# Attention with projected keys, then a two-branch maximum network: the loads of batch 0's v and of two weight matrices, each made in two transfers

## The chip, the core and the metric

The kernel runs on one core of a Trainium2 chip. A core has a matrix engine (TensorE, "PE" in the profile, with its weight loads as "PEld"), a vector engine (VectorE, "DVE"), a scalar engine (ScalarE, "ACT"), GpSimd ("POOL") and a queue engine (SyncE, "SP"). SP, ACT and POOL also issue transfers between the chip's memory and the on-chip memory (SBUF, 128 partitions); sixteen DMA engines carry them out. The metric is the device time of one execution in microseconds, as the median of several runs.

## What is computed

Eight batches of eight heads, 1,024 positions, head size 64. Keys and values are projected along the positions to 64 rows by E and F, softmax attention follows, and its output goes through two matrices, an elementwise maximum, and a third matrix:

```python
k_proj = np.einsum('ks,bhsd->bhkd', E, k)
v_proj = np.einsum('ks,bhsd->bhkd', F, v)
scores = scale * np.matmul(q, k_proj.transpose(0, 1, 3, 2))
scores = scores - np.max(scores, axis=-1, keepdims=True)
attn = np.exp(scores)
attn = attn / (np.sum(attn, axis=-1, keepdims=True) + 1e-09)
attn_out = np.matmul(attn, v_proj)
...
h1 = x @ w1
h2 = x @ w2
g = np.maximum(h1, h2)
return (g @ w_out).astype(np.float32)
```

x is the attention output as 8,192 rows of 512; w1 and w2 are 512 x 1,024, w_out is 1,024 x 512. All inputs are float32 in memory.

## The kernel before

The kernel computes in float16. The maximum is rewritten: max(h1, h2) = relu(h1 - h2) + h2, so that the second layer is relu(x wd) w_out + x m, with wd = w1 - w2 (`step_wd`, `step_wd_rows`) and m = w2 w_out (`m_steps`). For m, w2 is first transposed on TensorE (`step_w2t`). From batch 1 on, the products are made by a scheme of seven smaller products in place of eight, for which sums and differences of blocks are prepared on VectorE (`sums_x`, `sums_g`, `step_t`, `step_tw`).

The work is laid out by hand in one order for all engines; each engine runs its own instructions in the order in which they were written, and waits where data is missing. The batch is the outer unit. Batch 0 is the fill: its attention is done piece by piece while its inputs and the weights come in, with idle matmuls (`warm`) in the first 18 us to keep TensorE busy.

The loads of q, k, v and of the weights are issued from GpSimd, since they turn float32 into float16 on their way. They stand in this order: two heads of k are fetched by SP; then from GpSimd the other two heads of the first half of k, the first half of q, the second half of k, the second half of q; then batch 0's v in four loads of two heads (256 KB in SBUF each); then fourteen loads of pieces of w2 and w1 (128 KB each, two of them 256 KB), here called chunks 0 to 13; then w_out (1 MB), and batch 1's k, v, q and batch 2's k. Chunks 0 to 3 are columns 0 to 255 of w2 and w1, half of the rows each; 4 and 5 are columns 256 to 511 of w2, 6 and 7 the same of w1; 8 and 9 columns 512 to 1,023 of w2; 10 and 11 columns 512 to 767 of w1; 12 and 13 the rest of w1. A semaphore tells when a load has landed. GpSimd's loads use eight semaphores in turn.

How the loads are used: `step_kv` projects v (L195) as its four loads land. `step_wd` takes w1 - w2 of columns 0 to 255 from chunks 0 to 3 and of columns 256 to 511 from chunks 4 to 7 (DVE, L540); `step_wd_rows` does the columns from 512 on, one half of the rows at a time, from chunks 8 to 13 (L548). `up_slots` multiplies batch 0's x by wd, a block of 128 columns at a time (L524); `step_w2t` transposes w2 (L556), 256 columns at a time. Then `m_steps` needs w_out (L633), `step_t` makes its block differences (L596), and `down_steps` is the second layer (L837). Batch 1's k and v are projected at L237.

Of the kernel before, what the change touches and what calls it, by code (L numbers as in the profile page):

```python
# [19 lines left out]
def kernel(  # L20
# [12 lines left out]
    nc = tc.nc  # L33
# [5 lines left out]
    NC = S // 128  # L39
# [25 lines left out]
    def mm_bank(dtype=FP32, n=None):  # L65
        if n is None:
            n = turn.pop(0)
            turn.append(n)
        return ps.tile([128, 512 if dtype == FP32 else 1024], dtype, tag=f"mm{n}", name="mm_ps")
# [37 lines left out]
    def load(t, n, src, b, h0, h1):  # L107
        nc.gpsimd.dma_start(  # L108
            out=t[n][:, h0:h1],
            in_=src[b, h0:h1].rearrange("h (p c) d -> p h c d", c=NC),  # L110
        )

    tiles = {b: {} for b in range(B)}
    for n in ("k", "q", "v"):
        alloc(tiles[0], n)
# [4 lines left out]
                ident = const.tile([128, 128], FP32)  # L120
                make_identity(nc, ident)
    for h in range(0, H, 2):
        load(tiles[0], "v", v, 0, h, h + 2)

    w1_sb = big(1).rearrange("p (r f) -> p r f", r=NDC)
    w2_sb = big(2).rearrange("p (r f) -> p r f", r=NDC)
    wo_sb = const.tile([128, NFB, DM], FP16, tag="wo", name="wo_sb")
    for g in range(2):
        for w_sb, w in ((w2_sb, moe_w2), (w1_sb, moe_w1)):
            nc.gpsimd.dma_start(  # L130
                out=w_sb.rearrange("p (g z) f -> p g z f", z=2)[:, g, :, 0:256],
                in_=w.rearrange("(g p z) f -> p g z f", p=128, z=2)[:, g, :, 0:256],
            )
    for w_sb, w, f0, f1 in (
        (w2_sb, moe_w2, 256, 512), (w1_sb, moe_w1, 256, 512), (w2_sb, moe_w2, 512, DF),
        (w1_sb, moe_w1, 512, 768), (w1_sb, moe_w1, 768, DF),
    ):
        for z in range(2):
            nc.gpsimd.dma_start(
                out=w_sb.rearrange("p (g z) f -> p g z f", z=2)[:, :, z, f0:f1],  # L140
                in_=w.rearrange("(g p z) f -> p g z f", p=128, z=2)[:, :, z, f0:f1],
            )
    nc.gpsimd.dma_start(out=wo_sb, in_=moe_w_out.rearrange("(r p) f -> p r f", p=128))

# [866 lines left out]
    f = lambda s, *a: lambda: s(tiles[0], *a)  # L1011
# [72 lines left out]
    for n, x in enumerate((  # L1084
# [4 lines left out]
        for name in x.split():  # L1089
# [6 lines left out]
            else:  # L1096
                g, j = int(name[2]), int(name[3])
# [38 lines left out]
    for i, (new, old) in enumerate(zip([*groups[1:], none], groups)):  # L1136
        n, h = divmod(i + 2, 2)
# [54 lines left out]
    for reg in regs:  # L1192
# [4 lines left out]
        out=mm_bank()[0:1, 0:1], lhsT=ones16[:, 0:1], rhs=ones16[:, 0:1], start=True, stop=True  # L1197
# [166 lines left out]
```

## Time and profile before

| | us |
|---|---|
| median of 3 runs | 320.39 |
| lowest and highest run | 320.32, 322.92 |
| span of the profiled execution | 318.1 |
| TensorE busy in it | 312.3 |
| VectorE busy | 241.1 |
| ScalarE busy | 206.2 |
| GpSimd busy | 40.8 |

The span is the time from the first to the last instruction of one profiled execution; the runs' times are taken around it. The granted clock of TensorE was 1.000 over the span. The profile has these views: busy times by engine; the chain of work that ended last, followed backwards from the last instruction; windows, which give each engine's busy time in stretches of the span; timelines by engine; and, for a tile, its instructions, who waited for them, and how long its transfers took from issue to landing. In a timeline a row has its start, its length, engine, line, operation, the tile written and the one read, how many instructions are merged in it, and in brackets the idle time of the engine before it and what ended that. Several weight tiles appear under the name "big"; `v_sb`, `k_sb`, `q_sb` are the inputs, `wd_sb` is w1 - w2, `wo_sb` is w_out. The length of a transfer's row on GpSimd or SP is what the issue took, not the transfer. The DMA share is the mean busy share of the sixteen DMA engines, and exceeds 1 where packets overlap.

### The profile page before, as it was taken

The page shows a single profiled execution, that of the slowest core. Times are in us where ns is not written, and L with a number is a line of the kernel's source. Part 1 is how long each engine was busy: PE and PEld are TensorE (multiplying, and loading weights), DVE is VectorE, ACT ScalarE, POOL GpSimd, SP SyncE. Part 2 cuts the span into 40 slices and gives each one's busy share as a digit, 9 for nine tenths or more (in the row PEclk, how much of TensorE's full clock was granted, in tenths as well). Part 3 has the DMA queues.
Part 4 walks back from the last instruction along what each step waited for, and adds up shares of the span by engine and source line. Part 5 has one row for each costly group of instructions (what it writes and reads, how often), then busy time and mean ns, then how long its engine had stood idle before and what let it go on. Part 6 is the DMA issues. An engine that isn't in the chain of part 4 may idle for free.

```text
span 318.1 us, 9308 instructions
## 1 busy us (share of the span) xinstructions
PE 312.3 (98%) x3922; PEld 253.6 (80%) x3922; DVE 241.1 (76%) x441; ACT 206.2 (65%) x373; POOL 40.8 (13%) x63
## 2 busy tenths in 40 slices
PE   8989999999999999999999999999999999999996
PEld 3555588888887888788887888788887888888885
DVE  2366888877969696996969696996969696969883
ACT  2476842777776777477776778477776777765541
POOL 8259002003000300022000400030000000000000
PEclk9999999999999999999999999999999999999999
DMA  7999999999979999899999999989979131313124
GB/s 189 206 200 195 207 206 202 207 158 160 204 139 195 162 212 245 210 182 154 223 233 217 167 204 245 215 151 183 232 149 209 45 102 36 102 35 102 36 99 136
DMA packets 76684, 53.71 MB, mean 169 GB/s; under 512 B 29664, under 2 KB 76128, under 8 KB 76640
## 3 DMA queue, kind: packets, MB, share of 16 engines
q0 software_dynamic: 30688, 28.05, 56.0%
q1 hardware_dynamic: 45664, 24.85, 32.7%
q8 instruction: 31, 0.51, 0.6%
q10 hardware_dynamic: 288, 0.20, 0.2%
q14 instruction: 13, 0.11, 0.1%
HBM read 57.15 MB, written 16.78 MB: 232 GB/s over the span
## 4 chain that ended last, share of the span: by engine, by line
PE 92%; DMA 5%; POOL 1%; ACT 1%; issue 0%; DVE 0%; POOLq 0%
PE mm_ps L837 47%; PE mm_ps L745 27%; PE mm_ps L524 4%; DMA v_sb<-in_v_dram 4%; PE att_ps L352 3%; PE mm_ps L195 3%; PE mm_ps L340 2%; PE mm_ps L633 2%; PE att_ps L237 1%; DMA out_dram<-o_sb 1%; PE mm_ps L311 1%; POOL k_sb L108 0%; POOL q_sb L108 0%; ACT ld_sb L388 0%; ACT ex_sb L380 0%
## 5 line engine op out<-in xcount | busy, mean ns | idle before, releaser
L719 ACT COPY p_sb<-mm_ps 128x512 f32<-128x512 f32 x179 | 101.8, 592 | 49.1 <-PE mm_ps L745 27.2
L837 PEld LDWEIGHTS <-big 128*128 128x128 f16 x768 | 73.5, 98 | 11.8 <-issue 3.6
L837 PE MATMUL mm_ps<-T_sb,big 128*128 128x256 f16 x576 | 76.9, 273 | 0.0
L760 DVE TENSOR_TENSOR gt_sb<-mm_ps,p_sb 128x512 f16<-128x512 f32 x56 | 38.5, 687 | 43.0 <-PE mm_ps L745 41.6
L745 PE MATMUL mm_ps<-big,big 128*128 128x256 f16 x336 | 50.4, 273 | 0.0
L745 PEld LDWEIGHTS <-big 128*128 128x128 f16 x448 | 43.8, 98 | 5.1
L837 PE MATMUL mm_ps<-wo_sb,gt_sb 128*128 128x256 f16 x256 | 42.6, 273 | 0.0
L837 PEld LDWEIGHTS <-gt_sb 128*128 128x128 f16 x376 | 35.7, 98 | 6.7 <-issue 2.7
L469 ACT ACTIVATE ex_sb<-mm_ps 128x512 f16<-128x512 f32 x50 | 27.2, 596 | 18.0 <-PE mm_ps L340 12.3
L745 PEld LDWEIGHTS <-wd_sb 128*128 128x128 f16 x336 | 32.9, 98 | 3.8
L745 PE MATMUL mm_ps<-xt_sb,wd_sb 128*128 128x256 f16 x224 | 32.8, 273 | 0.0
L499 DVE TENSOR_TENSOR xt_sb<-att_ps,ld_sb 128x1024 f16<-128x1024 f32 x26 | 31.7, 1219 | 0.2
L837 PE MATMUL mm_ps<-m_sb,xt_sb 128*128 128x256 f16 x128 | 24.4, 273 | 0.0
L303 POOL COPY junk<-qt_sb 1x1 f16<-1x1 f16 x6 | 2.1, 346 | 172.5 <-DMA qt_sb<-q_sb 172.5
L868 DVE TENSOR_TENSOR o_sb<-mm_ps,p_sb 128x512 f32<-128x512 f32 x32 | 21.9, 683 | 2.8 <-ACT p_sb L897 2.0
L763 DVE TENSOR_SCALAR gt_sb<-gt_sb 128x512 f16<-128x512 f16 (+1 forms) x60 | 20.9, 348 | 2.1
L705 DVE TENSOR_TENSOR big<-gt_sb 128x1024 f16<-128x1024 f16 x32 | 21.8, 683 | 0.0
L837 PE MATMUL mm_ps<-wo_sb,big 128*128 128x256 f16 x128 | 21.5, 273 | 0.0
L806 ACT ACTIVATE gt_sb<-mm_ps 128x512 f16<-128x512 f32 x28 | 16.8, 601 | 5.7 <-PE mm_ps L745 5.7
L837 PE MATMUL mm_ps<-T_sb,gt_sb 128*128 128x256 f16 x120 | 20.3, 273 | 0.0
L837 PEld LDWEIGHTS <-xt_sb 128*128 128x128 f16 x188 | 18.3, 98 | 2.3 <-issue 0.2
L760 DVE TENSOR_TENSOR gt_sb<-p_sb 128x512 f16<-128x512 f32 x28 | 19.1, 682 | 0.6 <-ACT p_sb L719 0.6
(121 smaller groups left out, 434.7 us busy)
## 6 DMA issues: line engine op xcount, KB each, us to landing
out_dram<-o_sb SPq DMA_DIRECT2D x62, 256.0 KB
k_sb<-in_k_dram POOLq DMA_DIRECT2D x7, 1024.0 KB, 9.8
v_sb<-in_v_dram POOLq DMA_DIRECT2D x7, 1024.0 KB, 15.3
q_sb<-in_q_dram POOLq DMA_DIRECT2D x5, 1024.0 KB, 23.0
q_sb<-in_q_dram POOLq DMA_DIRECT2D x6, 512.0 KB, 15.8
big<-in_moe_w_dram POOLq DMA_DIRECT2D x12, 128.0 KB, 6.3
v_sb<-in_v_dram POOLq DMA_DIRECT2D x4, 256.0 KB, 13.6
wo_sb<-in_moe_w_out_dram POOLq DMA_DIRECT2D x1, 1024.0 KB, 10.4
```

The costliest lines, as they stand in the source:

```text
L195: nc.tensor.matmul(out=kv_ps[r * KP : (r + 1) * KP, h * D : (h + nh) * D], lhsT=eft[i][:, c, :], rhs=t[w][:, h0 + h : h0 + h + nh, c, :], ...
L469: nc.scalar.activation(out=t["ex", g, j][:, e, :], in_=banks[e], func=ACTF.Exp, scale=scale)
L499: nc.vector.tensor_tensor(out=x_out(t, g, j).rearrange("q z o n -> q o z n"), in0=at_ps.rearrange("q o (z n) -> q o z n", z=2), in1=ld[:, ...
L524: nc.tensor.matmul(out=h_ps, lhsT=wd_sb[:, r, fb * 128 : (fb + 1) * 128], rhs=t["xt"][:, r, :, j * W : (j + 1) * W], start=(r == 0), stop= ...
L705: nc.vector.tensor_tensor(out=S(i), in0=S(0) if x is None else x, in1=y(), op=op)
L719: copy(out=x, in_=bank)
L745: nc.tensor.matmul(out=bank[:, m * W : (m + 1) * W], lhsT=w_[:, n_, (2 * d + m) * 128 : (2 * d + m + 1) * 128], rhs=a[:, n_, :], start=(n ...
L760: nc.vector.tensor_tensor(out=c_blk(j, c), in0=two(x), in1=two(y), op=ALU.add)
L763: nc.vector.tensor_scalar_max(ap, ap, 0.0)
L806: nc.scalar.activation(out=out, in_=in_, func=ACTF.Relu)
L837: nc.tensor.matmul(out=bank[i][:, 0:CH] if two_banks else bank[:, i * CH : (i + 1) * CH], lhsT=a(c)[:, i * 128 : (i + 1) * 128], rhs=w_(c) ...
L868: nc.vector.tensor_tensor(out=o_sb, in0=two(x), in1=two(y), op=ALU.add)
```

## The change

A helper `load_parts` makes a load as two transfers: of partitions 0 to 119, and of partitions 120 to 127. Batch 0's v and all chunks of w1 and w2 go through it. Their order, and all other loads, are as before. The four loads of v become eight, the fourteen chunks twenty-eight transfers. Lines below the helper move down by 8 (those between by less).

```diff
+    SPLIT = 120
+
+    def load_parts(out, in_):
+        for p in slice(0, SPLIT), slice(SPLIT, 128):
+            nc.gpsimd.dma_start(out=out[p], in_=in_[p])
+
...
     for h in range(0, H, 2):
-        load(tiles[0], "v", v, 0, h, h + 2)
+        load_parts(
+            tiles[0]["v"][:, h : h + 2], v[0, h : h + 2].rearrange("h (p c) d -> p h c d", c=NC)
+        )
...
     for g in range(2):
         for w_sb, w in ((w2_sb, moe_w2), (w1_sb, moe_w1)):
-            nc.gpsimd.dma_start(
-                out=w_sb.rearrange("p (g z) f -> p g z f", z=2)[:, g, :, 0:256],
-                in_=w.rearrange("(g p z) f -> p g z f", p=128, z=2)[:, g, :, 0:256],
+            load_parts(
+                w_sb.rearrange("p (g z) f -> p g z f", z=2)[:, g, :, 0:256],
+                w.rearrange("(g p z) f -> p g z f", p=128, z=2)[:, g, :, 0:256],
             )
     for w_sb, w, f0, f1 in (
         (w2_sb, moe_w2, 256, 512), (w1_sb, moe_w1, 256, 512), (w2_sb, moe_w2, 512, DF),
         (w1_sb, moe_w1, 512, 768), (w1_sb, moe_w1, 768, DF),
     ):
         for z in range(2):
-            nc.gpsimd.dma_start(
-                out=w_sb.rearrange("p (g z) f -> p g z f", z=2)[:, :, z, f0:f1],
-                in_=w.rearrange("(g p z) f -> p g z f", p=128, z=2)[:, :, z, f0:f1],
+            load_parts(
+                w_sb.rearrange("p (g z) f -> p g z f", z=2)[:, :, z, f0:f1],
+                w.rearrange("(g p z) f -> p g z f", p=128, z=2)[:, :, z, f0:f1],
             )
```

## The prediction

> **What bounds the kernel now.** I read the page first, for the engine that is full and the chain that ends last.
>
> ```profile
> span 318.1 us, 9308 instructions
> PE 312.3 (98%) x3922; PEld 253.6 (80%) x3922; DVE 241.1 (76%) x441; ACT 206.2 (65%) x373; POOL 40.8 (13%) x63
> PE 92%; DMA 5%; POOL 1%; ACT 1%; issue 0%; DVE 0%; POOLq 0%
> ```
>
> TensorE carries nine tenths of the chain. Whatever makes it wait is added to the end, and nothing later gives it back. The rest of the chain is mostly the fill, which is also where every edited load lies. So the second view is the chain in order of time, and the third the windows of 5 us (columns: length, busy time of PE, its loads, DVE, ACT and POOL, granted clock, DMA share, GB/s).
>
> ```profile
> 5.54 13.33 DMA v_sb<-in_v_dram
> 18.92 0.64 PE mm_ps L195 x16
> 39.20 6.11 PE mm_ps L633 x56
> ```
>
> ```profile
> 20.00:25.00 5.00, 4.26 (x115) 2.59 (x111) 4.51 (x10) 3.24 (x6) 3.94 (x6) 1.00 1.44 196
> 25.00:30.00 5.00, 5.00 (x37) 2.63 (x35) 2.12 (x4) 4.29 (x7) 4.37 (x7) 1.00 1.33 196
> 30.00:35.00 5.00, 5.00 (x37) 2.76 (x36) 3.64 (x8) 3.69 (x7) 2.57 (x3) 1.00 1.28 203
> ```
>
> Until v's second load at 18.9 us the chain hangs on a transfer; from 25 us on TensorE has no gap at all. The DMA engines are full throughout (share over 1) at some 200 GB/s. So there is little to win after 25 us, and a good deal to lose: the weights arrive in just this stretch. How they are fed is in the timeline of POOL, which issues them (start, length, instruction, and in brackets the idle time before it with what ended it).
>
> ```profile
> 1.26 0.83 POOL L108 DMA_DIRECT2D k_sb<-in_k_dram  x1 [0.80 <-POOLq L1348]
> ...
> 4.86 2.84 POOL L108 DMA_DIRECT2D v_sb<-in_v_dram  x4
> 7.64 0.70 POOL L130 DMA_DIRECT2D big<-in_moe_w_dram  x1
> 10.60 0.71 POOL L130 DMA_DIRECT2D big<-in_moe_w_dram  x1 [2.25 <-DMA q_sb<-in_q_dram]
> 13.11 0.70 POOL L130 DMA_DIRECT2D big<-in_moe_w_dram  x1 [1.81 <-DMA k_sb<-in_k_dram]
> 15.65 0.71 POOL L130 DMA_DIRECT2D big<-in_moe_w_dram  x1 [1.84 <-DMA q_sb<-in_q_dram]
> 18.27 0.70 POOL L139 DMA_DIRECT2D big<-in_moe_w_dram  x1 [1.92 <-DMA v_sb<-in_v_dram]
> 19.16 0.71 POOL L139 DMA_DIRECT2D big<-in_moe_w_dram  x1 [0.19 <-issue]
> 20.43 0.70 POOL L139 DMA_DIRECT2D big<-in_moe_w_dram  x1 [0.56 <-DMA v_sb<-in_v_dram]
> 21.75 4.96 POOL L139 DMA_DIRECT2D big<-in_moe_w_dram  x7 [0.62 <-DMA v_sb<-in_v_dram]
> 26.80 0.88 POOL L143 DMA_DIRECT2D wo_sb<-in_moe_w_out_dram  x1
> 28.69 0.87 POOL L108 DMA_DIRECT2D v_sb<-in_v_dram  x1
> ```
>
> Two things are to be seen. First, an issue costs POOL about 0.7 us however little it moves. Second, a load waits for the landing of the load eight before it: the first weight chunk is the ninth load of the queue, the second waits for q (the second load), the third for k, the fourth for q, the fifth for the first v. The program's list of instructions says the same: eight semaphores in turn. Eight loads ahead were enough here to keep the engines full.
>
> Next, who needs the chunks. I number them 0 to 13 in order of issue; 4 is the one issued at 18.27, 7 the first of the row at 21.75. From DVE's and PE's timelines:
>
> ```profile
> 27.02 0.69 DVE L540 TENSOR_TENSOR wd_sb<-big,big 128x1024 f16<-128x1024 f16 x1 [0.89 <-DMA big<-in_moe_w_dram]
> 30.92 0.42 DVE L548 TENSOR_TENSOR wd_sb<-big,big 128x512 f16<-128x512 f16 x1 [0.18 <-DMA big<-in_moe_w_dram]
> ```
>
> ```profile
> 26.37 0.61 PE L556 MATMUL att_ps<-ident,big 128*128 128x128 f16 x8
> 26.82 4.58 PE L524 MATMUL mm_ps<-xt_sb,wd_sb 128*128 128x512 f16 x20
> 31.23 1.06 PE L556 MATMUL mm_ps<-ident,big 128*128 128x128 f16 x16
> 32.13 7.07 PE L524 MATMUL mm_ps<-xt_sb,wd_sb 128*128 128x512 f16 x32
> 49.41 0.39 PE L237 MATMUL att_ps<-v_sb,eft 128*64 128x256 f16 x4
> ```
>
> The difference w1 - w2 of columns 256 to 511 waits for chunk 7 (27.02) and ends at 27.71. Of the 20 matmuls from 26.82 on (0.22 us apart) the first four don't need it, and the fifth stands at 27.7. That gate has no slack.
>
> **What the change costs on POOL.** Four v loads become eight and fourteen chunks twenty-eight: 18 more issues, each a load of its own in the changed program's list of instructions. What does an issue of eight rows cost? No load on POOL in this trace has under 128 partitions. The nearest rows are on SP: the copies of 4 rows into the tile of sums, beside the one of 128 partitions.
>
> ```profile
> L396 SPq DMA_DIRECT2D checked<-ld_sb x32: 496/520/984, 16.8 to 286.5; - x32
> L87 SPq DMA_DIRECT2D kf_sb<-in_k_dram x1: 567/567/567, 1.4 to 1.4; - x1
> L108 POOL DMA_DIRECT2D q_sb<-in_q_dram x2: 760/764/769, 2.6 to 4.1; - x2
> ```
>
> On SP, 4 rows cost 0.52 us and 128 rows 0.57: the price is fixed. On POOL, 2 pieces per partition cost 0.71 (4.96 / 7), 4 pieces 0.76 and 8 pieces 0.88 (wo). That line through 0.71 and 0.88 meets no pieces at 0.65. I take 0.65 for the eight rows; the ends are 0.05 (were the price all by partition, 8/128 of 0.71) and 0.83 (the first load on POOL). A pair then costs 0.71 + 0.65 = 1.36 us, where a chunk cost 0.71.
>
> The waits move too. Eight loads ahead are now four pairs. The pieces of v's third and fourth pair wait for k, q, k and q: by the four landings above they are issued at 7.6, 10.6, 13.1 and 15.65 us. Their bytes stand behind the first v in the queue, and the fourth v landed just before 21.75, so they are still in time. No v is lost by it. But chunk 0, issued at 7.64 before, now waits for v's first piece. With v landing as before, that is 18.27. Before, five chunks were already in the queue or going into it at this moment; now none is.
>
> So pair n starts at 18.27 + 1.36n and its second piece 0.71 later. From there to landing a short transfer needs the start-up of the queue. A bound is a k load onto an idle queue (issue at 142.3):
>
> ```profile
> DMA to landing us min/median/max: 8.9/8.9/8.9
> DMA packets 1462, 1.45 MB, mean 207 GB/s; under 512 B 23, under 2 KB 1462, under 8 KB 1462
> ```
>
> The second row is the stretch from 31 to 38 us, full queue. 1.05 MB at 207 GB/s are 5.1 us, so start-up and completion take 3.8. The lower end is 0.65, the issue alone. I take 2.9, nearer the row, a little less because a fed queue isn't cold, and 0.1 for the few bytes: a pair lands 3.0 after its second issue starts.
>
> **The sum, gate by gate.** Chunks 4 and 5 feed the transposes at 26.37: pair 5's second issue is 18.27 + 6.8 + 0.71 = 25.8, landing 28.8, 2.4 late. Pair 7: 28.5, landing 31.5, and 0.69 of DVE: 32.2 instead of 27.7. That is +4.5 on TensorE, the 2.4 within it. Pair 11: 33.9, landing 36.9, DVE done at 37.4. The second matmul after 32.13 needs it, at 32.35 + 4.5 = 36.85: +0.5, together +5.0. Chunks 12 and 13 are needed 16 matmuls later, and come in time. w_out: issued at 18.27 + 14 x 1.36 = 37.3, landing 2.9 + 5.1 later, 45.3. Before:
>
> ```profile
> DMA to landing us min/median/max: 10.4/10.4/10.4
> DMA to landing us min/median/max: 18.7/18.7/18.7
> ```
>
> Issued at 26.80, it landed at 37.2 (first row), 1.8 before L633 took it up at 39.03. Now that place is due at 39.03 + 5.0 = 44.0, and waits until 45.3: +1.3, together **+6.3 us**. What is late next is batch 1's v: it landed at 28.69 + 18.7 = 47.4 (second row), 10.2 after w_out at the full rate, so now at 55.5. It is needed at 49.41 + 6.3 = 55.7. It just comes, and costs nothing more. After that the loads are issued by what TensorE finishes, and move with it. The eighteen extra issues themselves delay nobody but the loads behind them on POOL, counted here. The split's second pieces load some DMA engines with 9 shares instead of 8 while v streams; 4 x 1.27 / 8 = 0.6 us on v, hidden behind the later gates.
>
> 318.1 + 6.3 = 324.4 of the span; the median of the three runs, 320.39, is 2.3 above the span, so 326.7. With the start-up between 0.65 and 3.8 w_out lands at 43.1 to 46.2, and this case alone spans 324.4 to 327.6.
>
> **Rivals.** *The late DMA engine is dodged.* The landings of q, k, q in POOL's rows follow each other by 2.5 us for 512 KB, so the first v of 256 KB was due 1.27 after 15.65, at 16.92; it came at 18.27, 1.35 late, and the later ones stay 1.3 apart. In the stretch from 5 to 18 us there was one fetch of instructions:
>
> ```profile
> q8 instruction: 1, 0.02, 0.5%
> ```
>
> 0.5% of 16 engines x 13 us is 1.04 us, if one engine carries it all. A load lands with its last engine. If that engine has no share in the 120 rows, v's first piece lands 1.35 earlier, and all issues start at 16.92: +6.3 - 1.35 = +5.0, 325.4. For it speaks the lag itself; against it, that no view names the engine. The Trainium skill, "DMA: Bandwidth & Descriptors" (section on latency and other measured facts), says that engines 7 and 15 are usually slower than the rest, and its section on why a DMA increments its semaphore by 16 that a transfer of 100 partitions went to engines 0 to 14: by these two, 120 rows at 8 each would leave out engine 15. The trace has a late engine but can't say which. Its rules for kernel authors speak the other way, that two transfers to disjoint partitions only share the same engines and should be one. Chance 0.22.
>
> *Cheap small issues.* At 0.2 us, between 0.05 and 0.65, a pair costs 0.91: pair 7 lands at 18.27 + 6.4 + 0.71 + 3.0 = 28.4, 1.4 behind the old gate, and w_out at 18.27 + 12.7 + 8.0 = 39.0 hides behind that. 321.8. For it: only that POOL shows no small load. Against it: SP's rows. Chance 0.15.
>
> *No slower, even faster.* Both at once, with an eight-row issue at nearly nothing: a pair costs 0.71 as a chunk did, from 16.92 on; pair 7 lands at 16.92 + 5.0 + 0.71 + 3.0 = 25.6, 1.3 before the old gate, and v's chain is up to 1.35 earlier too. Then 320.4 - 1.3 = 319.1. This decides only below about 0.1 us for the small issue. Chance 0.07. More than that can't be won, since TensorE is full from 25 us on.
>
> *Dearer issues.* If 120 rows don't divide as easily, and both pieces cost what the first load on POOL did, 0.83, a pair costs 1.66, and w_out is issued 14 x 0.30 = 4.2 later: 330.9. Chance 0.11.
>
> **How the numbers follow.** The forecast has 0.40, the rivals 0.22, 0.15, 0.07 and 0.11, and 0.05 is something else. The range from 321.5 to 330.5 holds the forecast, the first rival, most of the second and most of the fourth. 1% is 3.2 us, about what this measurement can tell from no change: over 1% faster no case reaches (0.03 for what I don't see); within it lie the cheap and the lucky case and a little of the others' lower ends, 0.26; the rest, 0.71, is slower.
>
> **What would show it.** In the changed profile POOL should run without a pause from about 18 to 38 us, in pieces of 0.65 to 0.7 us; w_out's issue should stand near 37 us and the DMA share between 21 and 38 us fall well under 1. DVE's wait before L540 should grow from 0.89 to about 5 us, TensorE should show gaps before chunks 5, 7 and 11 and before w_out, and from 56 us on be a copy of the old timeline, shifted. I am wrong if eight-row issues are far shorter, if chunk 0 goes out well before 17 us, or if TensorE waits somewhere after 60 us.

## The result, and the profile after

The changed kernel took 329.48 us (median of 4 runs, 328.28 to 329.85), the kernel before 320.36 beside it: a ratio of 1.0281, 95% interval 1.0257 to 1.0306, or 9.1 us more. The profiled execution has a span of 326.5 us and a granted clock of 1.000; it took 328.28 us. The other three runs had clocks of 0.988 to 0.994 and spans of 327.5 to 328.1. That belongs to the result, and comes back below.

The page of the changed kernel: span, busy times, and the shares of the chain that ended last.

```profile
span 326.5 us, 9341 instructions
...
PE 313.3 (96%) x3922; PEld 253.7 (78%) x3922; DVE 241.9 (74%) x441; ACT 206.7 (63%) x373; POOL 51.5 (16%) x81
...
PE 74%; DMA 19%; POOL 5%; issue 1%; DVE 0%; POOLq 0%
```

TensorE's busy time grew by 1.0 us, the span by 8.4: nearly all of the added time is waiting. POOL has the 18 more issues, and 10.7 us more of busy time. In the chain, TensorE's share fell from 92% to 74% and that of transfers rose from 5% to 19%.

POOL's timeline of the changed kernel (start, length, instruction; in brackets the idle time before it and what ended that):

```profile
13.71 0.74 POOL L117 DMA_DIRECT2D v_sb<-in_v_dram  x1 [2.00 <-DMA k_sb<-in_k_dram]
16.29 0.55 POOL L117 DMA_DIRECT2D v_sb<-in_v_dram  x1 [1.84 <-DMA q_sb<-in_q_dram]
17.58 1.28 POOL L117 DMA_DIRECT2D big<-in_moe_w_dram  x2 [0.73 <-DMA v_sb<-in_v_dram]
19.50 15.75 POOL L117 DMA_DIRECT2D big<-in_moe_w_dram  x24 [0.64 <-DMA v_sb<-in_v_dram]
35.93 1.31 POOL L117 DMA_DIRECT2D big<-in_moe_w_dram  x2 [0.68 <-DMA big<-in_moe_w_dram]
37.21 0.96 POOL L151 DMA_DIRECT2D wo_sb<-in_moe_w_out_dram  x1
```

The first two rows give the prices: 0.74 us for 120 partitions, 0.55 for eight. From 17.58 to 38.2 us GpSimd does nothing but issue, with two pauses of under 0.7 us. The w_out load goes out at 37.21 us instead of 26.80.

What that does to the transfers is in the windows (length; busy time of PE, its loads, DVE, ACT, POOL; granted clock, DMA share, GB/s):

```profile
20.00:25.00 5.00, 4.26 (x139) 2.69 (x135) 4.20 (x9) 3.38 (x6) 4.99 (x9) 1.00 0.93 120
25.00:30.00 5.00, 3.88 (x28) 1.84 (x26) 1.88 (x4) 2.85 (x4) 5.00 (x9) 1.00 0.90 110
30.00:35.00 5.00, 3.58 (x18) 1.58 (x17) 1.38 (x2) 2.44 (x5) 5.00 (x8) 1.00 0.95 119
```

Where the kernel before moved 196 to 203 GB/s, this one moves 110 to 120, while POOL is busy all 5 us of each stretch. The same bytes come in; they are asked for too late. TensorE has 3.88 and 3.58 us of work in stretches where it had 5.00. Its timeline, with DVE's below, shows what for:

```profile
28.66 0.55 PE L564 MATMUL att_ps<-ident,big 128*128 128x128 f16 x7 [0.40 <-DMA big<-in_moe_w_dram]
...
31.48 3.63 PE L532 MATMUL mm_ps<-xt_sb,wd_sb 128*128 128x512 f16 x16 [1.42 <-DVE wd_sb L548]
...
35.95 1.00 PE L564 MATMUL mm_ps<-ident,big 128*128 128x128 f16 x15 [0.78 <-DMA big<-in_moe_w_dram]
37.93 6.87 PE L532 MATMUL mm_ps<-xt_sb,wd_sb 128*128 128x512 f16 x31 [0.31 <-DVE wd_sb L556]
46.44 1.92 PE L641 MATMUL mm_ps<-wo_sb,big 128*128 128x256 f16 x16 [1.65 <-DMA wo_sb<-in_moe_w_out_dram]
57.28 1.06 PE L245 MATMUL att_ps<-v_sb,eft 128*64 128x256 f16 x16 [0.29 <-DMA v_sb<-in_v_dram]
80.90 0.41 PE L348 MATMUL mm_ps<-qt_sb,kpt_sb 64*32 64x256 f16 x16 [0.40 <-DMA qt_sb<-q_sb]
```

```profile
30.74 0.69 DVE L548 TENSOR_TENSOR wd_sb<-big,big 128x1024 f16<-128x1024 f16 x1 [2.85 <-DMA big<-in_moe_w_dram]
36.75 0.43 DVE L556 TENSOR_TENSOR wd_sb<-big,big 128x512 f16<-128x512 f16 x1 [2.63 <-DMA big<-in_moe_w_dram]
```

Read the starts against the kernel before. The transposes of chunk 5 go on at 28.66 instead of 26.37, after 0.40 us of waiting. The sixteen matmuls behind chunk 7 come at 31.48; the fifth of the 20 from 26.82 on stood at 27.7: +3.8. The 31 matmuls at 37.93 answer to 32.35: +5.6. The first matmul of w_out comes at 46.44 instead of 39.03: +7.4. Batch 1's v comes at 57.28 instead of 49.41: +7.9. After the last wait that the kernel before doesn't have, at 80.9, the old timeline runs 8.4 later to the end. So nearly nine tenths of the loss (7.4 of 8.4) are there by 46.4 us.

### The profile page after: what moved, and what is told of

It is laid out like the page before. It is cut to its first block, busy times and chain, and to the rows that moved or that the text cites. A ratio compares the mean times of both kernels' runs of the same rounds, so it can differ in the third digit from the quotient of the medians.

```text
span 326.5 us, 9341 instructions
## 1 busy us (share of the span) xinstructions
PE 313.3 (96%) x3922; PEld 253.7 (78%) x3922; DVE 241.9 (74%) x441; ACT 206.7 (63%) x373; POOL 51.5 (16%) x81
## 3 DMA queue, kind: packets, MB, share of 16 engines
q0 software_dynamic: 31552, 28.06, 55.5%
## 4 chain that ended last, share of the span: by engine, by line
PE 74%; DMA 19%; POOL 5%; issue 1%; DVE 0%; POOLq 0%
PE mm_ps L845 41%; PE mm_ps L753 25%; DMA v_sb<-in_v_dram 10%; DMA q_sb<-in_q_dram 5%; POOL big L117 4%; PE mm_ps L203 3%; PE att_ps L360 3%; PE mm_ps L348 2%; DMA big<-in_moe_w_dram 2%; DMA qt_sb<-q_sb 2%; DMA out_dram<-o_sb 1%; POOL k_sb L108 1%; POOL q_sb L108 0%; POOL v_sb L117 0%; PE att_ps L245 0%
## 5 line engine op out<-in xcount | busy, mean ns | idle before, releaser
L771 DVE TENSOR_SCALAR gt_sb<-gt_sb 128x512 f16<-128x512 f16 (+1 forms) x60 | 21.6, 359 | 2.1
L845 PEld LDWEIGHTS <-xt_sb 128*128 128x128 f16 x188 | 18.3, 98 | 2.3 <-issue 0.2
## 6 DMA issues: line engine op xcount, KB each, us to landing
q_sb<-in_q_dram POOLq DMA_DIRECT2D x5, 1024.0 KB, 22.9
```

The costliest lines, as they stand in the source:

```text
L771: nc.vector.tensor_scalar_max(ap, ap, 0.0)
L845: nc.tensor.matmul(out=bank[i][:, 0:CH] if two_banks else bank[:, i * CH : (i + 1) * CH], lhsT=a(c)[:, i * 128 : (i + 1) * 128], rhs=w_(c) ...
```

## The experiments

The two theories were these. *Issues*: GpSimd needs about the same time for every issue, the doubled issues delay each load behind them, and the time follows from when w_out and chunk 7 go out. *Shape*: the unequal pieces themselves are slow, for instance because eight partitions occupy few DMA engines, whatever the number of issues. Differences are to the kernel before on the same chip (320.13 us for the first four runs, 320.03 for the next four, 319.98 for the last).

**Only v split.** Against the changed kernel, with lines below the helper 3 further down, as in most of these kernels:

```diff
+    def load_whole(out, in_):
+        nc.gpsimd.dma_start(out=out, in_=in_)
...
-            load_parts(
+            load_whole(
                 w_sb.rearrange("p (g z) f -> p g z f", z=2)[:, g, :, 0:256],
...
-            load_parts(
+            load_whole(
                 w_sb.rearrange("p (g z) f -> p g z f", z=2)[:, :, z, f0:f1],
```

> Only batch 0's v is split, the weight chunks are whole. Theory of issues (each extra issue holds GpSimd 0.55 to 0.74 us, and the eight semaphores reach only half as far ahead): four more issues, all of them before 18 us, where the DMA queue is full; the weights are issued back to back from 17.6 us on and w_out near 28 us instead of 37.2. Median 320.5 to 321.5. Theory of shape (a transfer of 120 rows is itself slow): v would land later by a us or more, and the weights be as before; 321 to 322. This run alone does not separate them, it bounds v's part.

Measured: 321.92 us, ratio 1.0046 (1.0025 to 1.0067), +1.8: a little above what the issues gave, and within the shape's range. Two of the ten runs, at 319.84 and 320.20, were no slower than the kernel before. TensorE's timeline in the profiled one (321.72):

```profile
20.04 0.64 PE L206 MATMUL mm_ps<-v_sb,eft 128*64 128x128 f16 x16 [1.37 <-DMA v_sb<-in_v_dram]
...
29.59 3.63 PE L535 MATMUL mm_ps<-xt_sb,wd_sb 128*128 128x512 f16 x16 [0.63 <-DVE wd_sb L551]
```

It waits 1.37 us for the second load of v, taken up at 20.04 where the kernel before had it at 18.92: 1.1 us late. Then it waits once more, 0.63 us for chunk 7, and the sixteen matmuls behind that start at 29.59 instead of 27.7: 1.9 us late. Chunk 7's load went out at 23.40 instead of 21.75, because chunks 2 to 7 all had to follow the second v's landing (issued from 19.88 on), while the kernel before had four chunks out by 16.4. The first matmul of w_out comes 1.8 us late, at 40.85, without a wait of its own. So the second wait is the one that ends last: the split of v costs 1.8 us alone, of which 1.1 were there at v and the rest came with chunk 7, and none by a delayed w_out.

**Only the chunks split.**

```diff
     for h in range(0, H, 2):
-        load_parts(
+        load_whole(
             tiles[0]["v"][:, h : h + 2], v[0, h : h + 2].rearrange("h (p c) d -> p h c d", c=NC)
         )
```

> Only the weight chunks are split, v is whole. Theory of issues: two pairs are already out before v lands (their semaphores are those of k and q), so 24 issues of 0.64 follow 18.3 us; w_out is issued near 33.6 us, lands near 42.7, and the time rises by about 4 us: 324 to 325.5. The two halves of the change then do not add up: together they cost 9 because v's split uses up the semaphores. Theory of shape: the 120-row weight transfers are what is slow, so all of the loss stays: 328 to 329.5.

Measured: 327.42 us, ratio 1.0221 (1.0203 to 1.0239), +7.3: between the two. POOL's timeline:

```profile
21.75 12.51 POOL L117 DMA_DIRECT2D big<-in_moe_w_dram  x19 [0.58 <-DMA v_sb<-in_v_dram]
34.57 1.31 POOL L117 DMA_DIRECT2D big<-in_moe_w_dram  x2 [0.30 <-DMA big<-in_moe_w_dram]
35.85 0.95 POOL L154 DMA_DIRECT2D wo_sb<-in_moe_w_out_dram  x1
```

The expectation overlooked that the loads behind v still wait for v's landings, as before: 21 issues are left after the fourth v at 21.75 us, so w_out goes out at 35.85. Part of the rest is in TensorE's timeline and in windows of 2 us:

```profile
31.86 5.26 PE L535 MATMUL mm_ps<-xt_sb,wd_sb 128*128 128x512 f16 x16 [3.27 <-DVE wd_sb L551]
```

```profile
31.00:33.00 2.00, 1.14 (x3) 0.44 (x4) 0.69 (x1) 0.00 (x0) 2.00 (x5) 0.70 0.80 119
33.00:35.00 2.00, 2.00 (x6) 0.76 (x5) 0.00 (x0) 0.60 (x1) 1.70 (x3) 0.50 1.27 166
```

After 3.27 us of waiting for chunk 7, the granted clock fell to 0.50, and the 16 matmuls took 5.26 us where the changed kernel's took 3.63. The wait costs more than its length.

The issues don't explain the whole of this wait. Chunk 7's second piece was issued at 26.99, 0.9 us earlier than in the changed kernel (27.93), and landed 0.5 us later. The trace has sixteen increments of a load's semaphore, as many as there are DMA engines, with the time of each. Of this piece's, fifteen came by 29.62 us and the last at 30.99; in the changed kernel fifteen came by 30.45 and the last at 30.46. Read as one increment for each engine, one engine was 1.4 us late. An estimate: without that the wait would have been 1.9 us, nearer to the 1.42 of the changed kernel. A fetch of instructions (16 KB, 1.0 us) began at 28.93; that it caused the delay isn't shown. The last increment of w_out was late too, 46.93 after 45.44. The two parts (1.8 and 7.3) happen to add up to the whole (9.1), but by different ways: the whole kernel's profile has neither the 1.37 nor the lower clock.

**All loads in halves of 64 and 64.** The same 18 more issues, equal pieces.

```diff
-    SPLIT = 120
+    SPLIT = 64
```

> As the changed kernel, but each load is cut into partitions 0 to 63 and 64 to 127, so that every engine has an equal share of each transfer. Theory of issues: the number of issues is the same, a pair costs about 1.3 us, and the time is that of the changed kernel, 328.5 to 330.5. Theory of shape: with even shares most of the loss goes, 320.5 to 323.

Measured: 326.21 us, ratio 1.0202 (1.0169 to 1.0235), +6.1: between the two ranges. POOL's timeline, then TensorE's:

```profile
18.54 15.99 POOL L117 DMA_DIRECT2D big<-in_moe_w_dram  x27 [1.48 <-DMA v_sb<-in_v_dram]
34.57 0.92 POOL L151 DMA_DIRECT2D wo_sb<-in_moe_w_out_dram  x1
```

```profile
43.83 1.92 PE L641 MATMUL mm_ps<-wo_sb,big 128*128 128x256 f16 x16 [1.00 <-DMA wo_sb<-in_moe_w_out_dram]
```

27 issues in 15.99 us are 0.59 each, where 24 unequal ones took 0.656 each. So w_out goes out 2.6 us earlier than in the changed kernel, and TensorE's first matmul of it comes 2.6 us earlier, each 9.2 us after the issue. Two thirds of the loss stay with equal pieces. The third that goes belongs to the shape, but by way of the issue: the issues are shorter, and their unbroken row starts 1 us earlier and has no pause.

**The eight rows once for each tensor.** All loads of 120 partitions, and the last eight rows of v, w2 and w1 in one transfer each ahead of them: 3 more issues.

```diff
-        for p in slice(0, SPLIT), slice(SPLIT, 128):
-            nc.gpsimd.dma_start(out=out[p], in_=in_[p])
+        nc.gpsimd.dma_start(out=out[0:SPLIT], in_=in_[0:SPLIT])
+
+    def load_tail(out, in_):
+        nc.gpsimd.dma_start(out=out[SPLIT:128], in_=in_[SPLIT:128])
...
+    load_tail(tiles[0]["v"], v[0].rearrange("h (p c) d -> p h c d", c=NC))
...
+    for w_sb, w in ((w2_sb, moe_w2), (w1_sb, moe_w1)):
+        load_tail(
+            w_sb.rearrange("p (g z) f -> p g z f", z=2), w.rearrange("(g p z) f -> p g z f", p=128, z=2)
+        )
```

> Rows 0 to 119 as in the changed kernel, but the last eight partitions of all of batch 0's v, of all of w2 and of all of w1 come in one transfer each, ahead of the others: 3 more issues than before, not 18. Theory of issues: 320.4 to 321.5. If the late DMA engine is dodged by the 120 rows, v's first load lands near 17 us instead of 18 and the time is 319.4 to 320.2. Theory of shape: the 120-row transfers are slow by themselves, 325 or more.

Measured: 323.68 us, ratio 1.0117 (1.0099 to 1.0135), +3.6; no expectation held. TensorE's timeline:

```profile
23.39 0.64 PE L213 MATMUL att_ps<-v_sb,eft 128*64 128x128 f16 x16 [0.77 <-DMA v_sb<-in_v_dram]
...
25.38 3.58 PE L542 MATMUL mm_ps<-xt_sb,wd_sb 128*128 128x512 f16 x8 [0.27 <-DVE wd_sb L558]
```

The fourth load of v is late (taken up at 23.39 instead of 21.66), and eight matmuls take 3.58 us instead of 1.90, at a granted clock of 0.66 in the stretch from 25 to 30. Few issues, and still slower: the issues are not all of it. The run moved v and the weights at once, so the next four take this apart, with v whole in all of them.

**Only chunks 0 to 7 split** (columns 0 to 511), the later ones whole.

```diff
-            load_parts(
+            (load_parts if f0 < 512 and f1 <= 512 else load_whole)(
```

> Only weight chunks 0 to 7 are split; v and chunks 8 to 13 are whole. Theory of issues: up to chunk 7 this is the run with all chunks split, whose second piece of chunk 7 went out near 27 us, and TensorE waits as long for it (about 3.3 us, with the clock lowered for some matmuls behind that wait); w_out goes out near 32 us, 4 earlier, lands near 42 and delays nothing. L524 ends near 44.9 instead of 39.2, so +5 to +6: 325 to 326.5; if the clock stays up, 324. If instead w_out alone sets the loss, 321 to 322.

Measured: 326.32 us, ratio 1.0193 (1.0176 to 1.0210), +6.3. TensorE's timeline:

```profile
31.94 6.22 PE L535 MATMUL mm_ps<-xt_sb,wd_sb 128*128 128x512 f16 x16 [3.12 <-DVE wd_sb L551]
...
45.80 1.91 PE L644 MATMUL mm_ps<-wo_sb,big 128*128 128x256 f16 x16
```

The wait for chunk 7, with the lower clock after it (6.22 us for 16 matmuls), makes nearly the whole of the loss. Here too the last increment of chunk 7's second piece was 1.3 us late (31.07, after fifteen by 29.76). The w_out load, issued at 31.89, is in when TensorE gets there.

**Only chunks 8 to 13 split.**

```diff
-            load_parts(
+            load_whole(
                 w_sb.rearrange("p (g z) f -> p g z f", z=2)[:, g, :, 0:256],
...
-            load_parts(
+            (load_parts if f1 > 512 else load_whole)(
```

> Only weight chunks 8 to 13 are split. Theory of issues: chunk 7 goes out at 21.75 us and lands near 27 us as before; the twelve later issues of 0.655 push w_out from 26.8 to 30.3 us. The queue still has work at that time, so w_out lands about 10 us later, near 40.5, 1.5 behind its place at 39.03: +1 to +2.5, 321.3 to 322.8. Theory of shape: six 120-row transfers of fourteen, 3 or more.

Measured: 322.90 us (5 runs, 322.16 to 324.36), ratio 1.0091 (1.0063 to 1.0118), +2.9, a tenth of a us past what the issues gave and a tenth short of what the shape gave: the time doesn't separate them. POOL's and TensorE's timelines:

```profile
25.43 3.12 POOL L117 DMA_DIRECT2D big<-in_moe_w_dram  x5 [0.75 <-DMA big<-in_moe_w_dram]
28.78 2.58 POOL L117 DMA_DIRECT2D big<-in_moe_w_dram  x4 [0.23 <-issue]
31.36 0.92 POOL L154 DMA_DIRECT2D wo_sb<-in_moe_w_out_dram  x1
```

```profile
41.54 1.92 PE L644 MATMUL mm_ps<-wo_sb,big 128*128 128x256 f16 x16 [1.77 <-DMA wo_sb<-in_moe_w_out_dram]
```

Here w_out alone is the gate: issued 4.6 us later than before, it is waited for 1.77 us. It went out 1.1 us later than the sum of issues had it, since GpSimd also paused, at 25.43 for 0.75 us, until an earlier chunk had landed. The early chunks and the late ones cost 6.3 and 2.9 us alone and 7.3 together. They hang on two different gates, chunk 7 and w_out, and the second hides behind the first in part.

**v whole, the eight rows of w2 and w1 once each**: 2 more issues, v as before.

```diff
+    for w_sb, w in ((w2_sb, moe_w2), (w1_sb, moe_w1)):
+        load_tail(
+            w_sb.rearrange("p (g z) f -> p g z f", z=2), w.rearrange("(g p z) f -> p g z f", p=128, z=2)
+        )
```

> v whole; the chunks are of rows 0 to 119, and the last eight partitions of w2 and of w1 come in one transfer each ahead of the chunks: 2 more issues than before. Theory of issues: chunk 7 goes out about 1.5 us later, near 23.2 us, and w_out near 28.2; +0.3 to +1.2, 320.5 to 321.4. Theory of shape (120 rows are slow to move): 322.5 or more, with the rate of the DMA engines between 21 and 30 us under the 196 GB/s of before though the queue is full.

Measured: 323.52 us, ratio 1.0123 (1.0085 to 1.0161), +3.5, as the shape would have it. A window and TensorE's timeline:

```profile
20.00:25.00 5.00, 2.89 (x110) 2.02 (x104) 3.00 (x7) 3.30 (x6) 2.57 (x4) 1.00 1.57 156
```

```profile
22.91 0.64 PE L212 MATMUL att_ps<-v_sb,eft 128*64 128x128 f16 x16 [1.18 <-DMA v_sb<-in_v_dram]
...
24.83 3.27 PE L541 MATMUL mm_ps<-xt_sb,wd_sb 128*128 128x512 f16 x8 [0.19 <-DVE wd_sb L557]
```

The fourth load of v, whole and issued as before, comes at 22.9 instead of 21.66. The DMA share is high (1.57), but only 156 GB/s come of it. The rate from 20 to 24 us, in 40 slices of 0.1 us:

```profile
GB/s 298 225 133 226 139 87 144 185 210 143 56 41 36 77 77 61 82 46 72 118 57 118 164 215 215 149 190 184 190 180 200 200 179 215 175 333 184 174 189 185
```

From 21.0 to 22.2 us it is 36 to 118 GB/s. The two small transfers, 64 KB each, were issued at 7.80 and 10.49 us, behind all four loads of v (4.87 to 7.71), so v doesn't stand behind them in the queue. Nor is half of the load late: of the sixteen increments of v's fourth load, fourteen came by 20.79 us, one at 21.39 and the last at 22.87, where the kernel before had fifteen by 20.48 and the last at 21.47. What slows the engines in this stretch stays open. The eight matmuls then start at 24.83 instead of 23.32 and take 3.27 us instead of 1.90, and the first matmul of w_out comes 3.3 us late, at 42.33, which is the whole loss. So an effect exists that the number of issues doesn't explain, in the two runs that fetch eight rows of a whole matrix at once. The changed kernel doesn't show it: there the low rate goes with a low share (0.93 at 120 GB/s), not with a high one.

**v whole, the chunks in halves.** SPLIT is 64, and v goes through load_whole.

```diff
-    SPLIT = 120
+    SPLIT = 64
...
-        load_parts(
+        load_whole(
             tiles[0]["v"][:, h : h + 2], v[0, h : h + 2].rearrange("h (p c) d -> p h c d", c=NC)
```

> As the run in which only the chunks are split, but into partitions 0 to 63 and 64 to 127. An issue of 64 rows took 0.59 us, those of 120 and 8 rows 0.74 and 0.55. Theory of issues at these prices: 21 issues after the last v landing save 0.06 each, w_out goes out near 34.5 instead of 35.9 us; the wait for chunk 7 falls under 3 us, and if the clock then stays up, another 1.6 us go: 324 to 325.5, against 327.4 with 120 and 8. If the price of an issue does not matter, 327 to 328.

Measured: 326.12 us, ratio 1.0182 (1.0165 to 1.0200), +6.1: between the two ranges. POOL's and TensorE's timelines:

```profile
22.02 12.49 POOL L117 DMA_DIRECT2D big<-in_moe_w_dram  x21 [0.83 <-DMA v_sb<-in_v_dram]
34.62 0.92 POOL L154 DMA_DIRECT2D wo_sb<-in_moe_w_out_dram  x1
```

```profile
31.32 5.31 PE L535 MATMUL mm_ps<-xt_sb,wd_sb 128*128 128x512 f16 x16 [2.49 <-DVE wd_sb L551]
```

The w_out load went out at 34.62 us, 34.5 by the price of the issues. But 2.49 us of waiting were again followed by a lower clock (5.31 us for 16 matmuls), which the sum by issues had not counted on. (Of chunk 7's second piece, fifteen increments came by 29.57 and the last at 30.45.)

**Three transfers for each chunk**, of 112, 8 and 8 partitions; v whole. 14 more issues than with the chunks in two, the same bytes: the run that pulls the theories furthest apart.

```diff
-        for p in slice(0, SPLIT), slice(SPLIT, 128):
+        for p in slice(0, 112), slice(112, SPLIT), slice(SPLIT, 128):
...
-        load_parts(
+        load_whole(
             tiles[0]["v"][:, h : h + 2], v[0, h : h + 2].rearrange("h (p c) d -> p h c d", c=NC)
```

> The v loads stay whole and each chunk of w2 and w1 is made in three transfers, of 112, 8 and 8 rows: 14 more issues than where only the chunks are split in two, the same bytes. If the issues on GpSimd set the time: sixteen loads are out when the fourth v lands at about 21.75 us, and 34 more follow at 0.60 on average (0.71, 0.55 and 0.55), so the w_out load is issued at about 42.2 us, against 35.85 with the chunks split in two; it lands 9.2 to 11.1 later, at 51.4 to 53.3, and TensorE's first matmul of w_out starts 12.4 to 14.3 us after the 39.03 of the kernel before: 332.5 to 335 us. If it is the uneven shape of the transfers (eight rows that go to few engines) and not their number, the small transfers carry 16 rows instead of 8 and the gates move by little: 327 to 329.5 us, as where the chunks alone are split in two (327.42).

Measured: 334.13 us, ratio 1.0443 (1.0426 to 1.0461), +14.2. POOL's and TensorE's timelines:

```profile
21.64 20.50 POOL L117 DMA_DIRECT2D big<-in_moe_w_dram  x35 [0.64 <-DMA v_sb<-in_v_dram]
42.09 0.97 POOL L154 DMA_DIRECT2D wo_sb<-in_moe_w_out_dram  x1
```

```profile
51.01 1.92 PE L644 MATMUL mm_ps<-wo_sb,big 128*128 128x256 f16 x16 [2.22 <-DMA wo_sb<-in_moe_w_out_dram]
```

The issue theory's numbers were 42.2 us for w_out's issue, 51.4 to 53.3 for its first matmul, 332.5 to 335 in all; 42.09, 51.01 and 334.13 came out. The matmul comes 0.4 us before its range, because w_out took 8.9 us to land, less than the 9.2 to 11.1 of the sum. Up to it 12.0 us are lost; the other 2.0 of the span come later, 0.8 of them in a wait for batch 1's v, and the sum didn't have them: that the total agrees is luck in part. The shape theory's 327 to 329.5 falls.

The five kernels in which TensorE waited for w_out, beside the kernel before, in the order of its first matmul (us):

| kernel | w_out issued | to landing | its first matmul | span |
|---|---|---|---|---|
| before | 26.80 | 10.4 | 39.03 (no wait) | 318.1 |
| chunks 8 to 13 split | 31.36 | 10.1 | 41.54 | 321.0 |
| all in halves | 34.57 | 9.2 | 43.83 | 323.5 |
| the change | 37.21 | 9.2 | 46.44 | 326.5 |
| chunks in two, v whole | 35.85 | 11.1 | 46.98 | 326.8 |
| chunks in three, v whole | 42.09 | 8.9 | 51.01 | 332.1 |

From the second row to the last, 10.7 us more at the issue are 9.5 at the first matmul and 11.1 in the span. The 11.1 us with the chunks in two include the late increment told of above: fifteen of the sixteen were in after 9.6. No version tried beats the kernel before; its TensorE has no gap from 25 to 35 us, where the weights arrive, so there was nothing for a split to win there. (Later it has one wait of 1.2 us, for an output transfer, so the prediction's "no gap at all" holds for that stretch only.)

## Why the prediction was right, and what was mis-sized

The mechanism of the forecast held, and the time of 329.48 us lies in its range of 321.5 to 330.5. It is 2.8 us above the point, 326.7. The steps in order:

- *A pair costs 1.36 us.* The two pairs that the profile shows singly took 1.28 and 1.31. Both pieces were a little off the other way round: 0.74 for the 120 partitions, dearer than the 0.71 of a whole chunk, and 0.55 for eight instead of 0.65. Of the bounds 0.05 and 0.83 for the small issue, the row of 4-partition transfers on SP (0.52) was the better guide than the line through POOL's own larger loads.
- *Pair 0 starts at 18.27, w_out goes out at 37.3.* 17.58 and 37.21. That the end agrees to 0.1 us is luck. The start was 0.7 us earlier, and the issues of the fourteen pairs took 18.3 us (1.28 + 15.75 + 1.31) instead of 19.0; but GpSimd paused twice, 0.64 us for the second v and 0.68 us for chunk 9, and the sum had no pause.
- *Chunk 5's gate at 28.8, chunk 7's +4.5 us.* The transposes went on at 28.66. Chunk 7 cost +3.8: DVE started at 30.74 where a landing at 31.5 was forecast: from the second issue (27.93) to landing (30.46) it took 2.5 us, not 3.0.
- *Chunk 11's gate, together +5.0.* +5.6, but not as the sum had it. The transposes of w2's later columns waited 0.78 us for chunk 9, which the sum didn't list as a gate at all. It reckoned 3.0 us from a pair's second issue to landing for every chunk, and this term was too short behind chunk 7. Chunks 8 and 9 are twice as large, and in the stretch from 30 to 46 us the second pieces took this long (count, KB each, median us from issue to landing), the last row being chunk 9's:

```profile
big<-in_moe_w_dram POOLq DMA_DIRECT2D x4, 8.0 KB, 4.0
big<-in_moe_w_dram POOLq DMA_DIRECT2D x1, 16.0 KB, 5.3
```

- *w_out 8.0 us from issue to landing, +6.3 in all.* 9.2 us, and +7.4. This is the largest term that was mis-sized. The start-up was taken as 2.9 us, "a little less because a fed queue isn't cold". In fact the queue was hardly fed. The bytes moved from 30 to 46 us, in 40 slices of 0.4 us:

```profile
GB/s 42 38 105 187 182 123 79 100 111 123 148 155 181 177 165 136 131 90 58 135 132 31 15 113 77 90 169 202 205 187 184 205 189 205 207 202 212 195 133 123
```

Slices 22 and 23, from 38.4 to 39.2 us, move 31 and 15 GB/s, just after w_out's issue, and the full rate is back from 40.8 on, 3.6 us after the issue. The idle queue's own 3.8, the upper end of that term, was the right choice. It also needs 5.6 us from there, not 5.1.
- *Batch 1's v just comes, and costs nothing.* It was forecast for 55.5 and needed at 55.7; it was taken up at 57.28. TensorE waited 0.29 us and lost 0.46 (7.87 against 7.41); batch 2's q cost 0.4 at 80.9. The margin of 0.2 us depended on w_out being in at 45.3; once that term was short, this one was too. The forecast's sign of error, a wait after 60 us, occurred, with 0.4 us.
- *v loses 0.6 us, hidden behind the later gates.* The first matmuls with wd start 0.6 us later (23.93 against 23.32), and chunk 7's gate hides that. But the second half of q, which the change doesn't touch, had landed 0.6 us later already (16.02 against 15.37). So the trace doesn't show that the uneven shares are the reason.
- *The signs.* w_out's issue near 37 us came true. POOL ran from 17.6 us on as forecast, though not without a pause: it had the two above. DVE's wait for chunk 7 grew to 2.85 us, not to 5, since its work before came later too. The DMA share fell to 0.90 to 0.95, not "well under 1", with 40% less moved: it is the GB/s that shows a starved queue.
- *Span and median.* The span came out 2.1 above the forecast's 324.4. The other 0.7 are outside the profiled execution: that one took only 1.8 more than its span, 0.5 less than reckoned, but the median run was 1.2 longer than it. All the other three runs had a lower mean clock (0.988 to 0.994). The profiled execution had none of that, so what happened in those runs is not seen; it fits the drops after long waits in the experiments.

The rivals. *The late engine is dodged*: no. There is a late engine, as the rival supposed: of the first v's sixteen increments in the kernel before, fifteen came by 16.69 us and the last at 17.98. In the changed kernel the first v has no such gap (its pieces were in at 17.29 and 17.45) and released GpSimd at 17.58 instead of 18.27. But the second v has one, and TensorE took it up later than before (19.53 against 18.92). With v alone split, the second v's piece of 120 partitions had fifteen increments by 18.10 and the last at 19.59, and TensorE waited 1.37 us for it. So the piece without the last eight partitions is held up too; which engine it is, no view says. (The prediction had the later v loads 1.3 us apart. In the trace the second lands 0.9 after the first, at 18.88, so the lag shrinks to about 1 us.) *Cheap small issues* and *no slower* needed 0.2 and 0.1 us; 0.55 was measured. *Dearer issues* needed 0.83 for both pieces; it didn't happen, though the time came near it by the other terms.

The Trainium skill, "DMA: Bandwidth & Descriptors" (Rules for kernel authors), which the prediction set against this change, advises one transfer of 128 partitions in place of two to disjoint partition halves, since both halves share the same engines. The advice agrees with the runs, that in halves of 64 and 64 included (6.1 us slower). The reason isn't what these runs show: here the time went mainly with GpSimd's issues.

## What to carry to other kernels

Before splitting a transfer, count the issues of its queue in the stretch where it feeds the critical engine: here a GpSimd issue cost 0.55 to 0.74 us whether it moved eight partitions or 120, so by this estimate pieces of about 60 to 128 KB can't be asked for as fast as the engines move them (128 KB at 200 GB/s are 0.65 us). Once the issuing engine is the slower one, the load to look at is the last and largest behind the small ones, here w_out, and it pays the start-up of an almost idle queue on top of its delay. In a sum of this kind every consumer in the stretch belongs on the list with its own size of transfer, and a margin of 0.2 us that stands on an estimated term is no margin.

## What the hardware showed that was not expected

A wait of TensorE can cost more than its length. After waits of 2.49, 3.27, 3.12 and 3.60 us for chunk 7 (the last with three transfers for each chunk), sixteen matmuls took 5.31, 5.26, 6.22 and 6.47 us instead of 3.63, and the granted clock was down to 0.50 in 2 us windows. In the profiled executions of the change and of the halves, with longest waits for data of 1.65 and 1.88 us, it stayed at 1.00, and so it did over the waits of 2.06 and 2.22 us for w_out with the chunks in two and in three. But with the eight rows of the weights once each, the longest wait was 1.18, TensorE was busy only 2.89 of the 5 us before, and the clock fell as well: it isn't the length of one gap alone that decides. The Trainium skill, "TensorE: Matmul & The Clock Gate" (Part 1), says that the clock falls to half after at least one idle window of about 3.4 us, counted by a window that runs freely. The drop to 0.50 agrees; that it takes a gap of 3.4 us does not, by these runs.

A load can hang on one sixteenth of itself. The last of a load's sixteen increments came 1.3 us after the other fifteen at the first v of the kernel before, 1.5 at the second v where v alone is split, and 1.4, 1.3 and 0.9 at chunk 7 with the chunks in two, with only chunks 0 to 7 split and with the chunks in halves. Taken off the waits of 3.27, 3.12 and 2.49 us, these last three leave 1.9, 1.8 and 1.6, by an estimate: no longer than the 2.22 after which the clock stayed up. What makes one increment late wasn't tried.

A smaller issue isn't always cheaper: by partitions, 128 cost 0.70 to 0.71 us, 120 cost 0.74, 112 cost 0.67, 64 cost 0.59 and 8 cost 0.55. Why 120 are dearer than 128 was not tried.
